# Blocks 3 to 8 in pairs, the first product by Strassen's scheme, weight operands kept in DRAM

## The chip, the cores and the metric

The kernel runs on one core of one Trainium2 chip. The metric is device microseconds of one execution. The core's engines are TensorE (PE, with its weight loads as PEld), VectorE (DVE), ScalarE (ACT), GpSimd (POOL) and SyncE (SP, which here only issues DMAs); each takes its instructions in program order and waits at an instruction until its semaphores allow it. PE writes to PSUM, eight banks of 128 x 512 fp32; DVE and ACT read and write both SBUF and PSUM.

## The reference

A linear attention feeds a gated feed-forward layer. Cut to what matters (q, k, v are 8 x 8 x 576 x 64, `d_model` is 512, `d_ff` is 1536):

```python
q_s = exp(q - max(q, -1)); q_s = q_s / (sum(q_s, -1) + 1e-09)
k_s = exp(k - max(k, 2));  k_s = k_s / (sum(k_s, 2) + 1e-09)
x = einsum('bhsd,bhde->bhse', q_s, einsum('bhsd,bhse->bhde', k_s, v))   # as [4608, 512]
xn = x / sqrt(mean(x * x, -1) + 1e-06) * rms_g
g = xn @ w_gate                                  # 512 -> 1536
out = (g * (1 / (1 + exp(-g))) * (xn @ w_val)) @ w_out   # 1536 -> 512
```

## The kernel before

The 4608 tokens are nine blocks j of 512 (`NB`, `TB`), the 1536 hidden features twelve chunks i of 128 (`NF`). A chunk of a block is a step s = 12 j + i. All three matrix products of the feed-forward layer are made in three passes over operands split in two fp32r parts, hi x hi, hi x lo and lo x hi, since one fp32r pass isn't exact enough.

For each s: `w_hi` casts the gate and val weights of the chunk (ACT, line 333), `w_lo` subtracts to get their low parts (POOL, line 811, one call for gate and one for val), `o_hi` and `o_lo` (line 819) do this for the out weights. `f1.s.0` and `f1.s.1` are gate and val: 12 matmuls each (4 slices of `d_model` x 3 passes, line 834) into one of two PSUM banks `ps_gv`. `g_mul` (DVE, line 839) multiplies the gate by the tokens' RMS factor r, `silu` (ACT, line 843) follows, `h_mul` (DVE, line 846) multiplies by val, `h_hi` (ACT) and `h_lo` (POOL, line 855) split the result, and `f2.s` (12 matmuls, line 873) adds its part of the out product to four PSUM banks `ps_o`, in which a block gathers over its 12 chunks. `store` scales by the RMS factor and writes the output. The weights come as 64-bit floats and are converted once, in block 0 (the `conv_` steps); the split into hi and lo is done anew for every s, 108 times, from the converted weights in `w_0` to `w_5`. The split tiles have two buffers each (`wsp`, `bufs=2`).

Beside this runs the attention: for batch b the `k_` steps make the 64 x 64 products of k and v, for block j the `q_` steps make softmax of q and its product with them, and the `x_` steps scale by `rms_g`, split and square the result; `n_` steps compute r. It uses two PSUM banks `ps_a`. All DMAs are issued by SP.

The order of everything is one string, `ORDER`: each word is a step with its numbers, and a letter behind a colon puts it on an engine (A is ACT, D is DVE, P is POOL). The program emits the steps in this order, and each engine gets its instructions in the order of emission.

Of the kernel before, what the change touches and what calls it, by code (L numbers as in the profile page):

```python
# [39 lines left out]
conv_low.1.0.2 n_sum0.2 conv_shift.1.1 q_max0.1.0 f1.0.0.0.2 conv_low.0.2.1 n_sum0.3 conv_sign.1.1 q_sub0.1.0:P  # L40
conv_low.2.0.2 f1.0.0.0.3 n_t.0 f1.0.1.0.0 f1.0.0.1.0 conv_add.1.0.2 f1.0.1.0.1 conv_mul.0.2 n_y0.0 f1.0.1.0.2
f1.0.1.0.3 f1.0.0.1.1 q_exp.1.0 conv_shift.0.2 f1.0.0.1.2 f1.0.0.1.3 conv_low.1.2.1 f1.0.1.1.0 n_y1.0 f1.0.1.1.1
f1.0.1.1.2 f1.0.1.1.3 f1.0.0.2.0 w_hi.1.0.2:A f1.0.0.2.1 f1.0.0.2.2 f1.0.0.2.3 f1.0.1.2.0 conv_low.3.0.2 conv_sign.0.2
w_lo.1.0:P f1.0.1.2.1 f1.0.1.2.2 f1.0.1.2.3 n_rows.0 k_tr.1.0 conv_low.2.2.1 conv_add.0.2.1 k_top.1.0 g_mul.0
# [890 lines left out]
```

## Time and profile before

| | |
|---|---|
| runs (us) | 1000.74, 1003.27, 1003.06; median 1003.06 |
| profiled execution: span | 1001.2 us |
| mean granted clock of PE | 0.997 |
| moved by DMA in the whole run | 56.71 MB on the data queue, mean 58 GB/s |
| written to DRAM | 9.44 MB |

The span is the time from the first to the last instruction of the one profiled execution; no other time of that execution is given, so the median stands 1.9 us above it for what lies around the span and for the spread of the runs. Block 0 with the loading and converting of the weights takes to about 130 us; after that a block takes 98 us plus the attention's matmuls. DMA traffic is heavy only in the first 100 us:

```profile
GB/s 236 239 305 172 116 44 88 29 52 35 44 57 42 39 1 77 47 42 16 77 35 35 35 54 57 36 35 23 65 27 9 1 43 1 1 1 42 1 1 43
```

Each number is one fortieth of the span, 25 us.

### The profile page before, as it was taken

What the parts mean: (1) busy time and instruction counts of PE and PEld (TensorE: products, weight loads), DVE (VectorE), ACT (ScalarE), POOL (GpSimd) and SP (SyncE); (2) the same over time, 40 slices, a digit from 0 to 9 for tenths busy, and PEclk for the clock granted to TensorE, in tenths of its full rate; (3) what the DMA queues carried; (4) which work ended last, traced back from release to release, by engine and by line L of the source; (5) the groups of instructions that cost most, each with busy time, mean ns of one, the idle gap of its engine ahead of it and who ended that gap; (6) DMA issues with size and microseconds to landing.
All of it is one profiled execution on the core that took longest, in us unless ns stands there. A gap on an engine that the chain in (4) does not pass through costs nothing.

```text
span 1001.2 us, 14424 instructions
## 1 busy us (share of the span) xinstructions
PE 987.5 (99%) x4897; PEld 799.2 (80%) x4897; DVE 486.6 (49%) x1170; ACT 602.7 (60%) x857; POOL 734.4 (73%) x640
## 2 busy tenths in 40 slices
PE   7999999999999999999999999999999999999998
PEld 5667878888888888888888888888888888888886
DVE  7978867654544445445444554544454322231111
ACT  5988678765765666655765666557665444434332
POOL 5688999987768786778676877777776767766663
PEclk9999999999999999999999999999999999999999
DMA  9795423121122102210211112110210010001001
GB/s 236 239 305 172 116 44 88 29 52 35 44 57 42 39 1 77 47 42 16 77 35 35 35 54 57 36 35 23 65 27 9 1 43 1 1 1 42 1 1 43
DMA packets 129686, 57.64 MB, mean 58 GB/s; under 512 B 101796, under 2 KB 123596, under 8 KB 129612
## 3 DMA queue, kind: packets, MB, share of 16 engines
q1 hardware_dynamic: 129612, 56.71, 21.7%
q8 instruction: 39, 0.64, 0.3%
q14 instruction: 35, 0.29, 0.1%
HBM read 47.25 MB, written 9.44 MB: 57 GB/s over the span
## 4 chain that ended last, share of the span: by engine, by line
PE 93%; POOL 3%; ACT 1%; DMA 1%; issue 1%; DVE 1%; SPq 0%; POOLq 0%; ACTq 0%
PE ps_gv L834 57%; PE ps_o L873 29%; PE ps_a L712 2%; PE ps_a L513 2%; POOL w L395 1%; DMA raw<-in_moe_w_out_dram 1%; PE ps_a L495 1%; DMA w<-in_k_dram 1%; POOL wl L811 0%; PE ps_a L762 0%; PE ps_a L481 0%; PE ps_a L641 0%; POOL ol L819 0%; PE ps_o L513 0%; DVE xl L734 0%
## 5 line engine op out<-in xcount | busy, mean ns | idle before, releaser
L811 POOL TENSOR_TENSOR wl<-w,wh 128x512 fp32r<-128x512 f32 x215 | 277.8, 1298 | 113.3 <-ACT wh L333 100.7
L834 PE MATMUL ps_gv<-xh,wh 128*128 128x512 f32 x864 | 346.0, 401 | 0.0
L834 PE MATMUL ps_gv<-xl,wh 128*128 128x512 f32 x864 | 336.9, 391 | 0.0
L834 PE MATMUL ps_gv<-xh,wl 128*128 128x512 f32 x864 | 231.6, 390 | 0.0
L839 DVE TENSOR_TENSOR gs<-ps_gv,r 128x512 f32<-128x512 f32 x108 | 74.6, 691 | 245.3 <-PE ps_gv L834 205.9
L834 PEld LDWEIGHTS ps_gv<-xh,wh 128*128 128x128 f32 x864 | 162.9, 189 | 36.8 <-issue 1.3
L834 PEld LDWEIGHTS ps_gv<-xh,wl 128*128 128x128 f32 x864 | 162.2, 188 | 34.9
L834 PEld LDWEIGHTS ps_gv<-xl,wh 128*128 128x128 f32 x864 | 162.9, 189 | 32.5 <-issue 0.6
L843 ACT ACTIVATE gs<-gs 128x512 f32<-128x512 f32 x108 | 68.3, 632 | 173.3 <-DVE gs L839 172.7
L873 PE MATMUL ps_o<-oh,hh 128*128 128x512 f32 x416 | 164.6, 396 | 0.0
L873 PE MATMUL ps_o<-ol,hh 128*128 128x512 f32 x416 | 162.2, 390 | 0.0
L855 POOL TENSOR_TENSOR hl<-gs,hh 128x512 fp32r<-128x512 f32 x104 | 134.5, 1293 | 28.8 <-ACT hh L333 28.3
L819 POOL TENSOR_TENSOR ol<-w,oh 128x512 fp32r<-128x512 f32 x104 | 134.6, 1294 | 16.3 <-ACT oh L333 16.3
L846 DVE TENSOR_TENSOR gs<-ps_gv,gs 128x512 f32<-128x512 f32 x108 | 74.6, 690 | 137.4 <-PE ps_gv L834 129.7
L333 ACT CAST wh<-w 128x1024 fp32r<-128x1024 f32 x103 | 108.0, 1049 | 48.8 <-PE ps_gv L834 44.7
L873 PE MATMUL ps_o<-oh,hl 128*128 128x512 f32 x416 | 111.9, 390 | 0.0
L333 ACT CAST oh<-w 128x512 fp32r<-128x512 f32 x104 | 64.0, 617 | 77.0 <-PE ps_o L873 74.7
L873 PEld LDWEIGHTS ps_o<-oh,hl 128*128 128x128 f32 x416 | 78.1, 188 | 16.7 <-POOL hl L855 0.2
L873 PEld LDWEIGHTS ps_o<-oh,hh 128*128 128x128 f32 x416 | 78.2, 188 | 16.4 <-issue 0.2
L873 PEld LDWEIGHTS ps_o<-ol,hh 128*128 128x128 f32 x416 | 78.2, 188 | 15.6 <-issue 0.2
L333 ACT CAST hh<-gs 128x512 fp32r<-128x512 f32 x103 | 64.0, 621 | 43.3 <-DVE gs L846 42.6
L843 ACT ACT_TABLE_LOAD x45 | 57.7, 1283 | 0.9
(147 smaller groups left out, 1082.8 us busy)
## 6 DMA issues: line engine op xcount, KB each, us to landing
out_dram<-ot SPq DMA_DIRECT2D x34, 256.0 KB
kt<-in_k_dram SPq DMA_DIRECT2D x28, 280.0 KB
vt<-in_v_dram SPq DMA_DIRECT2D x56, 140.0 KB
raw<-in_moe_w_gate_dram SPq DMA_DIRECT2D x7, 512.0 KB
raw<-in_moe_w_val_dram SPq DMA_DIRECT2D x7, 512.0 KB
raw<-in_moe_w_out_dram SPq DMA_DIRECT2D x7, 512.0 KB
w<-in_moe_w_gate_dram SPq DMA_DIRECT2D x5, 512.0 KB
w<-in_moe_w_val_dram SPq DMA_DIRECT2D x5, 512.0 KB
```

The costliest lines, as they stand in the source:

```text
L333: (e.copy if e is nc.scalar else e.tensor_copy)(dst, src)
L395: on(nc.gpsimd).tensor_tensor(out=dst, in0=dst, in1=raw_words(i, a, n, 0), op=ALU.add)
L513: nc.tensor.matmul(ps[h * D:(h + 1) * D, :D + 1], lhsT=ke[:n, h, j], rhs=vt[:n, j, h], start=(j == 0), stop=(j == len(rows) - 1))
L712: nc.tensor.matmul(px[:, c0:c1], lhsT=wt, rhs=mv[:, c0:c1], start=(i == 0), stop=(i == 2))
L811: on(nc.gpsimd).tensor_tensor(out=wl[:, a], in0=W(s % NF, a), in1=wh[:, a].bitcast(F32), op=ALU.subtract)
L819: on(nc.vector).tensor_tensor(out=ol, in0=W(s % NF, 2), in1=wo_[s][0].bitcast(F32), op=ALU.subtract)
L834: nc.tensor.matmul(pd[s], lhsT=m[:, a, c * P:(c + 1) * P], rhs=X[j, c][x], start=(n == 1), stop=(n == 3 * NKT))
L839: nc.vector.tensor_tensor(out=gs, in0=g_[s], in1=r_[s // NF], op=ALU.mult)
L843: nc.scalar.activation(g_[s], g_[s], AF.Silu)
L846: nc.vector.tensor_tensor(out=g_[s], in0=v_[s], in1=g_[s], op=ALU.mult)
L855: on(nc.gpsimd).tensor_tensor(out=hl, in0=g_[s], in1=h_[s][0].bitcast(F32), op=ALU.subtract)
L873: nc.tensor.matmul(po[t], lhsT=a[:, t * P:(t + 1) * P], rhs=w, start=(i == 0 and n == 0), stop=(i == NF - 1 and n == len(terms) - 1))
```

## The change

Blocks 0 to 2 are computed as before, with nearly the same steps up to s=11. Four things differ.

**Weights kept.** During blocks 1 and 2 (s=12 to s=25) the split weights are written to DRAM by SP: `w_keep` (two DMAs of 512 KB per s) and `o_keep` (two of 256 KB). For each pair of chunks four sums of weight blocks are formed, split and written too: `s_add`, `s_hi`, `s_lo`, `s_keep` (24 each, two DMAs of 256 KB each). In all 31.5 MB. Block 2 still splits its weights from `w_0` to `w_5`.

**Attention earlier.** The attention of blocks 3 and 4 is done in block 2, that of blocks 5 and 6 in pair 0, and so on, because a pair needs two blocks at once. `x_cp` makes the scaled copy, `x_nm` multiplies it by r before the product (so `g_mul` goes), and `t_add`, `b_hi`, `b_lo` build seven operands of two slices from four blocks (two halves of `d_model` x two token blocks), kept in the old weight buffers.

**Pairs.** Blocks 3 to 8 are three pairs p. A unit is a chunk pair i (of 6) and m (0 gate, 1 val). Per unit PE makes seven products `pp.p.i.m.k` of 6 matmuls in the order k = 1, 6, 5, 2, 7, 4, 3 into three PSUM banks A, B, C. A bank is read after each of its products, and the next product goes on adding to it: `c_s1` reads A after product 1, `c_u2` and `c_u3` B after 6 and 7, and `c_11`, `c_22`, `c_21`, `c_12` give the four results (two chunks x two token blocks). `gate` is the silu, `hm` the product with val, `hp_hi` and `hp_lo` the split, `f2p` the out product of one chunk and block (12 matmuls). The first block's `f2p` stands inside each unit, between products 7 and 4; the second block's twelve come one after another once the units are done. `put` stores without scaling.

**Weights read back.** In the pairs no weight is split. POOL issues DMAs that read the kept operands: per unit `w_in` part 1 (1 MB, line 1068, 128 x 2048) and part 2 (768 KB, 128 x 1536), and `o_in` (512 KB, line 1080) for each `f2p`; 144 DMAs. Part 1 has one buffer per m, part 2 one per m, the out weights four.

What moves is shown by the instruction rows of before and of the changed kernel (lines are those of each kernel's own file). On PE, the end of one chunk's first product and the start of an out product, near the end of before:

```order
L834 MATMUL ps_gv<-xl,wh 128x512
L834 MATMUL ps_gv<-xh,wl 128x512 [waits Pool_49]
L834 MATMUL ps_gv<-xh,wl 128x512 x3
L873 MATMUL ps_o<-oh,hh 128x512 [waits Activation_49]
L873 MATMUL ps_o<-ol,hh 128x512 [waits Pool_49]
```

And on PE in pair 1 of the changed kernel, products 5, 2, 7 of one unit and the `f2p` in it (`x_` tiles hold the operands, `ring_` tiles and `w` the weights read back, DMASW is a DMA issued by POOL):

```order
L1095 MATMUL ps_o<-x_4437,w 128x512 [waits DVE_49]
L1095 MATMUL ps_o<-x_4437,w 128x512 x5
L1095 MATMUL ps_o<-x_4199,w 128x512 [waits Activation_49]
L1095 MATMUL ps_o<-x_4199,w 128x512 x5
L1095 MATMUL ps_o<-x_4199,ring_3487 128x512 [waits DMASW3_49,DVE_49]
L1095 MATMUL ps_o<-x_4199,ring_3487 128x512
L1095 MATMUL ps_o<-x_4444,ring_3487 128x512 x2
L1095 MATMUL ps_o<-x_4199,ring_3487 128x512
L1095 MATMUL ps_o<-x_4444,ring_3487 128x512
L1182 MATMUL ps_a<-x_4170,hh 128x512 [waits DMASW5_49]
```

PE's waits for POOL's and ACT's weight splits are gone; in their place stand waits for DMAs and, at each product, for DVE or ACT having read the bank.

On POOL in block 1, a chunk or so before the change (`wl`, `ol`, `hl` are low parts, `qt` and `ql` attention):

```order
L811 TENSOR_TENSOR wl<-w_92,wh 128x512 [waits PE_49,Activation_49,Pool_49]
L855 TENSOR_TENSOR hl<-gs,hh 128x512 [waits Activation_49]
L811 TENSOR_TENSOR wl<-w_92,wh 128x512
L819 TENSOR_TENSOR ol<-w_92,oh 128x512 [waits Activation_49,Pool_49]
L664 TENSOR_TENSOR qt<-qt,st 128x512 [waits DMAHW3_49,DMAHW4_49,DMAHW2_49,DMAHW5_49,DMAHW1_49,DMAHW6_49,DMAHW0_49,DMAHW7_49,DVE_49,Pool_49]
```

And after it (line 877 is `w_lo`, 885 `o_lo`, 975 `h_lo`, 927 `s_add`, 936 `s_lo`; DMAHW is a DMA issued by SP):

```order
L975 TENSOR_TENSOR hl<-gs,hh 128x512 [waits Activation_49]
L936 TENSOR_TENSOR parts<-sums,parts 128x2x256 [waits DMAHW4_49,DMAHW3_49,Activation_49]
L877 TENSOR_TENSOR w<-w_93,w 128x2x256 [waits DMAHW1_49,DMAHW2_49,PE_49,Activation_49]
L516 MEMSET vt 116x10 [waits DMAHW6_49,DMAHW5_49,DMAHW7_49,DMAHW0_49,PE_49]
L936 TENSOR_TENSOR parts<-sums,parts 128x2x256 [waits DMAHW6_49,DMAHW5_49,Activation_49]
L885 TENSOR_TENSOR o<-w_92,o 128x512 [waits Activation_49]
L877 TENSOR_TENSOR w<-w_93,w 128x2x256 [waits DMAHW7_49,DMAHW0_49,Activation_49]
L877 TENSOR_TENSOR w<-w_93,w 128x2x256
L927 TENSOR_TENSOR sums<-sums,w_93 128x512
```

`s_add` and `s_lo` have come between the splits, and a split waits for the stores that read its buffer.

On DVE at the start of pair 0 (line 966 is `h_mul`, 733, 707, 737, 715 attention, 589 a reciprocal, 1014 `x_nm`, 1039 `t_add`, 1051 `b_lo`); in before this place has no such rows:

```order
L966 TENSOR_TENSOR gs<-ps_gv,gs 128x512 [waits PE_49,Activation_49]
L733 SCALAR_TENSOR_TENSOR sm<-sm,sw 128x16 [waits DVE_49]
L589 RECIPROCAL rs<-rs 128x1
L707 TENSOR_REDUCE sw<-st 32x16 x4
L737 RECIPROCAL sm<-sm 128x16 [waits DVE_49]
L715 TENSOR_TENSOR st<-st,sw 128x16 [waits DVE_49]
L1014 TENSOR_TENSOR xl<-xl,r 128x512
L1039 TENSOR_TENSOR ot<-xl,xh 128x512 [waits Pool_49] x2
L1039 TENSOR_TENSOR xl<-xl 128x512 [waits DVE_49,Pool_49]
L1039 TENSOR_TENSOR xl<-xl 128x512 [waits DVE_49]
L1039 TENSOR_TENSOR xh<-xl,xh 128x512 [waits DVE_49] x2
L1051 TENSOR_TENSOR x_4437<-ot,x_4437 128x512 [waits Activation_49]
```

The rows after it are four more of `b_lo`; PE's product 6 of the first unit waits for the third `b_lo`. Three of the four `x_nm` of block 4 stand on POOL.

The diff, cut to its core; of the `ORDER` string one line each of a late stretch is shown:

```diff
-store.6.3:A f1.86.0 h_mul.85 w_hi.87.0.2:A h_hi.85:A w_lo.87.0:P h_lo.85:P f2.84 g_mul.86 silu.86 w_lo.87.1:P f1.86.1
...
+c_u2.1.3.0 pp.1.3.0.2 pp.1.3.0.7 c_11.1.3.0 w_in.1.4.0.1 f2p.1.0.4 c_u3.1.3.0 c_22.1.3.0 gate.1.3.22 pp.1.3.0.4
...
+    wsp = ctx.enter_context(tc.tile_pool(name="wsp", bufs=2))
+    big = ctx.enter_context(tc.tile_pool(name="big", bufs=1))
...
+    S2, S1, A11, A12, A21, A22, S3, S4 = range(8)
+    wd = [[tc.dram_tile([P, 8, 2, HALF], F32, name=f"wd{i}_{m}") for m in range(2)] for i in range(NH)]
+    od = [tc.dram_tile([P, 2, DM], F32, name=f"od{i}") for i in range(NF)]
+    def w_keep(s):
+        i, odd = divmod(s % NF, 2)
+        at = A21 if odd else A11
+        for m in range(2):
+            nc.sync.dma_start(wd[i][m][:, at:at + 2], wh_[s][:, m].bitcast(F32))
+    def s_add(i, n):
...
+        c = turn["sums"] = turn.get("sums", -1) + 1
+        sums[i, n] = parts[0][:, c % 6]
+        x, y, op = {1: (a(1, 0), a(1, 1), ALU.add), 2: (sums.get((i, 1)), a(0, 0), ALU.subtract),
+                    3: (a(0, 0), a(1, 0), ALU.subtract), 4: (a(0, 1), sums.get((i, 2)), ALU.subtract)}[n]
+        on(nc.vector).tensor_tensor(out=sums[i, n], in0=x, in1=y, op=op)
+    def x_nm(j, g):
+        x = XF[(j - JP) % 2, g]
+        on(nc.vector).tensor_tensor(out=x, in0=x, in1=r_[j], op=ALU.mult)
+    def t_add(p, n, c):
...
+        o, x, y, op = {1: (T1.get(c), b, a, ALU.subtract), 3: (b, e, b, ALU.subtract), 2: (a, b, a, ALU.add),
+                       4: (d, d, a, ALU.subtract)}[n]
+        on(v).tensor_tensor(out=o, in0=x, in1=y, op=op)
+    def b_lo(p, o, c):
+        on(nc.gpsimd).tensor_tensor(out=operand(o, c, 1), in0=source(o, c), in1=operand(o, c, 0).bitcast(F32),
+                                    op=ALU.subtract)
+    def w_in(p, i, m, part):
+        ring()
+        if part == 1 and m == len(RING[1]):
+            RING[1].append(wsp.tile([P, 4, TB], F32R, name="w"))
+        t = RING[part][m].rearrange("p a b -> p (a b)")
+        src = wd[i][m][:, :4] if part == 1 else wd[i][m][:, 5:]
+        nc.gpsimd.dma_start(t, src.rearrange("p a b f -> p (a b f)"))
+    def o_in(p, t, c):
...
+        nc.gpsimd.dma_start(WO[n % 4], od[c])
+    PROD = {1: (A11, 0, 0), 6: (S2, 1, 1), 5: (S1, 2, 2), 2: (A12, 3, 0), 7: (S3, 4, 1), 4: (A22, 5, 1), 3: (S4, 6, 2)}
+    def pp(p, i, m, k):
+        w, o, b = PROD[k]
+        first = k in (1, 6, 5)
...
+        terms = [(0, c, x) for c in range(2) for x in range(2)] + [(1, c, 0) for c in range(2)]
+        for n, (h, c, x) in enumerate(terms):
+            nc.tensor.matmul(abc[b], lhsT=src[:, h, c * P:(c + 1) * P], rhs=operand(o, c, x),
+                             start=first and n == 0, stop=n == 5, skip_group_check=not first)
+    def combine(u, n, dst, src, b):
+        ux[u + (n,)] = dst
+        nc.vector.tensor_tensor(out=dst, in0=ux[u + (src,)], in1=abc[b], op=ALU.add)
+    def hm(p, i, n):
+        t = cell(p, i, n)
+        on(nc.vector).tensor_tensor(out=t, in0=t, in1=ux[p, i, 1, n], op=ALU.mult)
+    def f2p(p, t, c):
...
+        (hh, hl), (oh, ol) = HH[p, t, c], wo_[p, t, c]
+        terms = ((hh, oh), (hh, ol), (hl, oh))
+        order = [(n, k) for k in range(T) for n in range(2)] + [(2, k) for k in range(T)]
...
+    def put(p, t, n):
+        ot = fp.tile([P, DM], F32, name="ot", bufs=2)
+        copy(ot, pa[p, t, n], nc.vector if n % 2 else nc.scalar)
+        nc.sync.dma_start(ov[blk(p, t), n], ot)
```

More of the change, by code (lines that the diff above doesn't have):

```diff
@@ L40 @@
[L40 to L44, printed above, removed]
@@ L380, in conv_mul @@
     def conv_mul(i, a):
-        cv[i, a] = ps_a.tile([P, TB], F32, name="ps_a")
+        cv[i, a] = ps("attn")
         nc.scalar.mul(cv[i, a], raw_words(i, a, 1, 1).bitcast(F32), 2.0 ** -112)
@@ L397, in warm @@
     def warm(n, _=0):
-        out = ps_gv.tile([P, TB], F32, name="ps_gv")
+        out = ps("gv")
         for _ in range(n):
@@ L407, in attn_ps @@
     def attn_ps(first):
-        if first:
-            return ps_o.tile([P, TB], F32, name="ps_o")
-        return ps_a.tile([P, TB], F32, name="ps_a")
+        return ps("o" if first else "attn")
     kt_, vt_, ke_, mb_, cm_, kps, rs_, kv, kx_, kd_ = {}, {}, {}, {}, {}, {}, {}, {}, {}, {}
@@ L759, in n_sum @@
     def n_sum(j):
-        pm = ps_a.tile([P, TB], F32, name="ps_a")
+        pm = ps("attn")
         for i, a in enumerate(dg_[j]):
@@ new lines, in w_in @@
+    def w_in(p, i, m, part):
[6 more added lines that the diff above has]
+    def o_in(p, t, c):
+        ring()
+        n = turn["wo"] = turn.get("wo", -1) + 1
+        while len(WO) < 4 and n >= len(WO):
+            if len(WO) == 1:
+                operand(6, 1, 1)
+                WO.append(XO[4][:, 4:6])
+            else:
+                WO.append(wsp.tile([P, 2, DM], F32R, name="o"))
+        wo_[p, t, c] = [WO[n % 4][:, k] for k in range(2)]
+        nc.gpsimd.dma_start(WO[n % 4], od[c])
@@ new lines, in linear_attention_then_gated_ffn, with h2, c_s1 @@
+    ux = {}
+    def h2(c):
+        if c not in H2:
+            if c < 8:
+                H2[c] = xp.tile([P, TB], F32, name=("xh", "xl")[c // 4])
+            else:
+                t = wsp.tile([P, 4, TB], F32, name="w")
+                for k in range(4):
+                    H2[8 + k] = t[:, k]
+        return H2[c]
+    def c_s1(p, i, m):
+        t = ux[p, i, m, 1] = tmp("s")
+        copy(t, abc[0], nc.scalar)
+    def combine(u, n, dst, src, b):
+        ux[u + (n,)] = dst
+        nc.vector.tensor_tensor(out=dst, in0=ux[u + (src,)], in1=abc[b], op=ALU.add)
@@ new lines, in h_src, with hp_hi, hp_lo @@
+    def h_src(p, t, c):
+        return h2(c) if t else g_[p, c]
+    def hp_hi(p, t, c):
+        hh = fp.tile([P, TB], F32R, name="hh", bufs=2)
+        copy(hh, h_src(p, t, c), nc.scalar)
+        HH[p, t, c] = [hh]
+    def hp_lo(p, t, c):
+        hl = fp.tile([P, TB], F32R, name="hl", bufs=2)
+        on(nc.gpsimd).tensor_tensor(out=hl, in0=h_src(p, t, c), in1=HH[p, t, c][0].bitcast(F32), op=ALU.subtract)
+        HH[p, t, c].append(hl)
+    pa = {}
+    def f2p(p, t, c):
+        if c == 0:
+            if t and p + 1 < NPAIR:
+                attn_pool[0] = BANKS[p % 2][1][3]
+            for n in range(T):
+                pa[p, t, n] = ps(BANKS[p % 2][1 - t][n])
+        (hh, hl), (oh, ol) = HH[p, t, c], wo_[p, t, c]
+        terms = ((hh, oh), (hh, ol), (hl, oh))
+        order = [(n, k) for k in range(T) for n in range(2)] + [(2, k) for k in range(T)]
+        if c == NF - 1:
+            order.sort(key=lambda x: (x[1], x[0]))
+        for n, k in order:
+            a, w = terms[n]
+            nc.tensor.matmul(pa[p, t, k], lhsT=a[:, k * P:(k + 1) * P], rhs=w, start=(c == 0 and n == 0),
+                             stop=(c == NF - 1 and n == 2))
```

719 lines of the change are left out of this document (435 added, 284 removed).

## The prediction, made before the changed kernel had run

> **What bounds the kernel now.** I read the head of the page first, then its chain, then the chain's rows in order of time, then stretches of the run.
>
> ```profile
> span 1001.2 us, 14424 instructions
> PE 987.5 (99%) x4897; PEld 799.2 (80%) x4897; DVE 486.6 (49%) x1170; ACT 602.7 (60%) x857; POOL 734.4 (73%) x640
> PE 93%; POOL 3%; ACT 1%; DMA 1%; issue 1%; DVE 1%; SPq 0%; POOLq 0%; ACTq 0%
> ...
> 904.76 8.16 PE ps_gv L834 x36
> ...
> 986.36 5.44 PE ps_gv L834 x24
> ```
>
> TensorE (PE) is busy for 99% of the span and makes 93% of the chain that ends last. The chain rows give its pace: 36 matmuls in 8.16 us, so 0.2267 us each, and one feature chunk of a block (24 matmuls at L834, 12 at L873) takes 8.16 us. The stretches say what lies under it (columns: length, busy us of PE, PEld, DVE, ACT, POOL, then granted clock, DMA share, GB/s).
>
> ```profile
> 0.00:50.00 50.00, 42.74 (x234) 28.11 (x234) 40.52 (x97) 37.67 (x62) 29.18 (x52) 0.97 0.90 237
> 50.00:60.00 10.00, 8.02 (x47) 6.25 (x47) 7.10 (x13) 6.99 (x13) 7.66 (x6) 0.83 0.88 253
> 60.00:70.00 10.00, 10.00 (x38) 6.74 (x37) 8.43 (x14) 8.69 (x13) 7.57 (x8) 1.00 1.11 334
> 70.00:80.00 10.00, 10.00 (x40) 6.91 (x39) 9.16 (x15) 9.48 (x13) 10.00 (x8) 1.00 1.01 336
> 130.00:228.00 98.00, 98.00 (x509) 80.18 (x507) 62.56 (x168) 73.86 (x102) 88.78 (x78) 1.00 0.22 50
> 228.00:326.00 98.00, 98.00 (x510) 80.46 (x509) 50.86 (x130) 60.57 (x85) 73.20 (x63) 1.00 0.19 46
> 326.00:620.00 294.00, 294.00 (x1510) 241.36 (x1509) 141.20 (x373) 182.17 (x255) 216.86 (x186) 1.00 0.18 43
> ```
>
> From 130 us on PE has no gap at full clock. But in block 1 (about 130 to 228) POOL is already busy for 88.78 of 98 us, in block 2 for 73.20. So matmuls removed come off the end in full, while vector work added to blocks 1 and 2 meets a nearly full POOL.
>
> **The change part by part.** *Matmuls removed.* The first product of blocks 3 to 8 is 6 blocks x 12 chunks x 24 = 1728 matmuls; as seven half-size products it is 3 pairs x 12 units x 7 x 6 = 1512. 216 fewer x 0.2267 us = **-49.0 us**. The second product stays at 12 matmuls per chunk and block.
>
> *Vector work of the pairs.* In blocks 3 to 8 the three weight splits of each chunk go (three POOL operations of 1.30 us); per unit of 54 matmuls (12.24 us on PE) DVE now has some eight operations and POOL one or none.
>
> ```profile
> L811 POOL TENSOR_TENSOR wl<-w,wh 128x512 fp32r<-128x512 f32 x215 | 277.8, 1298 | 113.3 <-ACT wh L333 100.7 <-ACT hh L333 7.5 <-PE ps_a L762 3.1
> L846 DVE TENSOR_TENSOR gs<-ps_gv,gs 128x512 f32<-128x512 f32 x108 | 74.6, 690 | 137.4 <-PE ps_gv L834 129.7 <-PE ps_a L481 5.9 <-ACT wh L333 0.9
> L686 POOL TENSOR_TENSOR qt<-qt,sm 128x512 f32<-128x512 f32 x28 | 29.5, 1054 | 16.3 <-DVE sm L683 9.6 <-DVE rs L535 6.8
> L811 DVE TENSOR_TENSOR wl<-w,wh 128x512 fp32r<-128x512 f32 x1 | 0.7, 689 | 0.0
> ```
>
> Eight at 0.69 us are 5.5 of 12.24 us: PE covers them in pairs 1 and 2, and between a bank's last matmul and its next user lie two products, 2.72 us, for a read of 0.69. Cost nothing there. In pair 0 the attention of blocks 5 and 6 is added: counted with the row means, DVE has 135 us in eleven units of 151 us of PE, and over PE's time in four of them (2.0 us together). With the five build-up stages beside the second products, where x_nm and t_add make the next operands (about 4 us over), I take **+6**; the ends are 0 and 10.
>
> *Blocks 1 and 2 with the weights kept.* Here DVE and POOL disturb each other:
>
> ```profile
> 128.62 1.31 POOL L855 TENSOR_TENSOR hl<-gs,hh 128x512 fp32r<-128x512 f32 x1
> ...
> 129.21 1.27 DVE L739 TENSOR_TENSOR acc<-acc,sq 128x512 f32<-128x512 f32 x1
> ...
> 129.91 1.71 POOL L811 TENSOR_TENSOR wl<-w,wh 128x512 fp32r<-128x512 f32 x1
> ```
>
> The DVE sum of two SBUF tiles, 0.69 us alone, starts under a POOL operation and ends only 0.55 us after it; the POOL operation begun meanwhile takes 1.71 instead of 1.30. So the two kinds run as one queue. In block 1 (from the first product of s=12 to that of s=24) the new order has on POOL 68 such operations x 1.30 and 6 x 1.05 = 94.7 us, and on DVE 32 with two SBUF inputs x 0.69 = 22.1: 116.8 us against 106.8 of PE. That is 0 (if PE's work lies well around it) to 10; I take **+8**, since two weight buffers let POOL run only one chunk ahead. In block 2, 64 x 1.30 + 12 x 1.05 + 14 x 0.69 = 105.5 against 110.3, but DVE as a whole has 104.8, and in its first two chunks 25.4 against 22.4 of PE: 3.0, and as much again for the 14 shared operations waiting half a POOL operation (0.65, 9 us, a third of which has no slack): **+6**, ends 0 and 17 (the sum of every chunk's excess).
>
> The Trainium skill, "SBUF — State Buffer", section "Who interferes with whom", says that a DVE operation with two SBUF inputs and a POOL operation reading SBUF hold one port pair by turns and block each other; the trace agrees (1.27 against 0.689 us). Taken strictly, and for DVE casts too, it is the third case below.
>
> *The stores.* 31.5 MB leave over s=12 to 25, some 128 us: 246 GB/s, with the attention's 50 about 296. Loads reached 334 to 336, so I cost them nothing; the other end is the 237 of the first 50 us: 38 MB in 160 us, +32. SP issues 195 DMAs there:
>
> ```profile
> 61.44 4.00 SPq L455 DMA_DIRECT2D vt<-in_v_dram  x4
> ...
> 66.14 0.40 SPq L369 DMA_DIRECT2D w<-in_moe_w_gate_dram  x1
> ...
> 998.40 0.33 SPq L888 DMA_DIRECT2D out_dram<-gs  x1
> ```
>
> 0.33 to 1.0 us each, 64 to 195; near the middle row, which is a weight tile's (0.40 to 0.5), 90 of 128, hidden. Two waits are new. On SP the attention's loads stand behind a store that waits for its split; they come a chunk or more before use. On POOL a split waits until the store of two chunks earlier has read its buffer; behind it stands `h_lo`, for which the out product on PE waits. With some eight DMAs on the way at 88% of the rate a store is late now and then: that is in the +8 of block 1, whose cover is one chunk, 8.16 us.
>
> *The start of pair 0.* Product 6 needs both blocks normalised and added. From the end of the first product's gate half at s=35 DVE has in its queue: two PSUM products, two transposes, a sum, eight quarter moves and six small steps, then x_nm, six t_add and three b_lo.
>
> ```profile
> L839 DVE TENSOR_TENSOR gs<-ps_gv,r 128x512 f32<-128x512 f32 x108 | 74.6, 691 | 245.3 <-PE ps_gv L834 205.9 <-PE ps_a L481 15.3 <-POOL wl L811 13.4
> L691 DVE STREAM_TRANSPOSE qT<-qt 128x512 f32<-128x512 f32 x28 | 19.6, 702 | 1.3 <-POOL qt L686 1.2
> L672 DVE TENSOR_REDUCE sm<-qt 128x16 f32<-128x512 f32 x28 | 19.0, 679 | 15.6 <-ACT qt L668 15.6
> L653 DVE TENSOR_REDUCE sw<-sm 32x16 f32<-32x16 f32 x112 | 18.0, 161 | 2.1
> L535 DVE RECIPROCAL rs<-rs 128x1 f32<-128x1 f32 x32 | 4.9, 153 | 0.7
> L679 DVE SCALAR_TENSOR_TENSOR sm<-sm,sw 128x16 f32<-128x16 f32 x28 | 8.4, 299 | 0.3
> L683 DVE RECIPROCAL sm<-sm 128x16 f32<-128x16 f32 x28 | 7.1, 252 | 0.6
> ```
>
> 2 x 0.69 + 2 x 0.70 + 0.68 + 8 x 0.16 + 0.30 + 2 x 0.25 + three of about 0.16 = 6.0, and ten two-input operations x 0.69 = 6.9: ready 12.9 us on. PE has the value half (2.72) and product 1 (1.36), 4.1 us, so it stands for about 9. A stand is followed by slow matmuls:
>
> ```profile
> 56.28 0.86 PE L628 MATMUL ps_a<-ident,xl 128*128 128x128 f32 x4 [1.98 <-ACT ot L338]
> 56.80 0.77 PE L834 MATMUL ps_gv<-xh,wh 128*128 128x512 f32 x1
> ...
> 60.20 0.63 PE L834 MATMUL ps_gv<-xh,wl 128*128 128x512 f32 x2
> ```
>
> Eight matmuls in 3.40 us instead of 1.81, at a granted clock of 0.83 in that stretch: 1.6 more. Together **+10.7**; 4 if the steps before s=35 run ahead, 13 if POOL blocks half of those ten.
>
> *Weights read back.* POOL issues 144 DMAs, three per unit (2.36 MB in 12.24 us, 193 GB/s) and one of 0.52 MB per 2.72 us beside the second products, the same rate. No row shows a DMA issued by POOL: between nothing and SP's 1.0 us each, at most 3 of 12.24 us on a POOL that else has 1.3. I take nothing, because the rate is 58% of 334 to 336 and a buffer is refilled a unit ahead. The Trainium skill, "DMA: Bandwidth & Descriptors", section "Measured (HBM→SBUF, 128 partitions, SWDGE, issued from GpSimd)", gives 6.15 us and 341 GB/s for 1 MB; by it the term is nothing too, and no run here has shown it yet.
>
> *The end.* The last stores wait for the last matmuls as before: 0.
>
> **The sum:** 1001.2 - 49.0 + 8 + 6 + 10.7 + 6 = 982.9 by the span. The median of the runs, 1003.06, is 1.9 above the span: **985 us**, its own range 970 to 998.
>
> **The rivals.** *PE alone bounds:* the stalls hide, since the same PE queue had no gap beside a POOL at 91%; only part of the start of pair 0 is left. 1003.1 - 49.0 = 954, plus 0 to 14: 954 to 968. Against it stands the 12.9 us queue.
>
> *One queue of DVE and POOL throughout:* block 1 +12, block 2 +17, start +13, pair 0 and the build-ups +8: 1003.1 - 49 + 50 = 1004 at most, 996 to 1006 likely. For it: the stretched rows above. Against: in block 1 of before POOL and PE shared 98 us without a stop.
>
> *The read-back is too slow (slower than before):* all of the pairs' 104 MB come by POOL's queue while DVE and POOL work, and PE waits for a weight tile in each unit. PE needs 539 us for the pairs' weight matmuls; 104 MB in 560 us, 186 GB/s, is where the forecast passes 1006. At half the seen rate, 167, they take 622: 83 more, 1068. The Trainium skill, "SBUF — State Buffer", same section, warns that POOL's descriptor writing starves while DVE holds the pair; no row here shows it.
>
> *The products do not keep the pace:* 252 short groups with changing banks, each followed by a read. 18 us over 252 (0.07 us each) eats the gain; at 0.25, as in the few groups beside attention that take 2.97 instead of 2.72, it is 63 us and 1048.
>
> ```profile
> 723.62 2.97 PE ps_gv L834 x12
> 727.56 2.75 PE ps_gv L834 x12
> ```
>
> Against it: runs of 24 and 36 matmuls cross banks at 0.2267.
>
> **How the numbers follow.** Forecast 0.50, PE alone 0.17, one queue 0.18, slow read-back 0.11, lost pace 0.04. The forecast and PE alone are nearly all faster by over 0.3% (below 1000.0, about what a measurement here can tell from no change); the one-queue case is a third faster, two fifths the same, the rest slower; the last two slower. Faster 0.70, same 0.11, slower 0.19. A range from 954 to 1008 leaves out the last two cases and a little of the third, and covers the stores' dearer end (985 + 32 less the 14 already in blocks 1 and 2 = 1003).
>
> **What would show it.** PE busy near 938 us, 4,680 or so matmuls; PE at 2.72 us per 12 in pairs 1 and 2 with no gap named after a DMA; in blocks 1 and 2 gaps of PE ended by POOL or DVE (w_lo, g_mul, q_x inputs), some 14 us; one gap near 9 us at the first L1095 of pair 0, ended by DVE L1051, with a clock below 1 after it. A PE that waits for L1068 or L1080 loads in every unit would make it wrong, as would POOL rows of several us at L1068.

## The result, and the profile after

The changed kernel takes **1041.68 us** (median; 1037.83 to 1045.3) beside 1001.9 us of the kernel before on the same chip: a ratio of 1.0392, 95% interval 1.0358 to 1.0426. It is slower by about 39 us. The forecast was 985 us with a range of 954 to 1008: both the direction and the range were wrong.

The head of its page, and the first line of its chain:

```profile
span 1042.5 us, 14185 instructions
PE 971.2 (93%) x4681; PEld 773.5 (74%) x4681; DVE 739.7 (71%) x1460; ACT 467.3 (45%) x705; POOL 574.8 (55%) x575
PE 56%; DVE 20%; DMA 10%; issue 5%; POOL 3%; ACT 3%; SPq 3%; DVEq 0%; POOLq 0%; ACTq 0%
```

The 216 matmuls are gone (4897 to 4681). Their 49.0 us should have brought PE's busy time from 987.5 to 938.5; it is 971.2, since matmuls at half clock last longer (mean granted clock 0.967, before 0.997). And PE stands (has no matmul under way) for 1042.5 - 971.2 = 71.3 us, before for 13.7, which is 57.6 more. So the balance is -49.0 + 32.7 of slow matmuls + 57.6 of standing = +41.3 us of span. In the chain PE's share has fallen from 93% to 56%.

By stage (blocks 1 and 2, then the three pairs; columns as in the prediction: stretch, length, busy PE, PEld, DVE, ACT, POOL, granted clock, DMA share, GB/s), the changed kernel:

```profile
148.00:413.00 265.00, 240.51 (x1254) 191.11 (x1253) 228.23 (x477) 161.25 (x224) 204.38 (x175) 0.94 0.59 187
413.00:649.00 236.00, 214.76 (x1093) 171.92 (x1092) 192.69 (x429) 120.49 (x184) 141.59 (x145) 0.96 0.69 188
649.00:849.00 200.00, 189.22 (x823) 154.97 (x820) 114.56 (x189) 44.76 (x76) 72.50 (x84) 0.97 0.60 185
849.00:1042.00 193.00, 186.22 (x818) 152.80 (x816) 84.88 (x131) 24.96 (x41) 35.35 (x52) 1.00 0.57 177
```

PE stands for 24.5 us in blocks 1 and 2, for 21.2 in pair 0 and for 10.8 in pair 1, each time with a clock below 1. By the forecast the units of pair 1 should have had no gap. DVE is busy for 228 of 265 us in the first stage; in blocks 1 and 2 of before it had 113 of 196, less than ACT and POOL.

**What holds PE up.** The waits view of the changed kernel (engine, tile and line <- what it waited for: us in all, times, longest) has four rows on one tile, the buffer through which a block's result leaves:

```profile
DVE ot L389 <- DMA out_dram<-ot: 21.4, 5, 5.7
ACT ot L389 <- DMA out_dram<-ot: 21.4, 4, 9.6
...
DVE ot L396 <- DMA out_dram<-ot: 14.5, 4, 7.5
...
ACT ot L394 <- DMA out_dram<-ot: 13.8, 3, 6.0
```

These are 71 us in 16 waits, of two engines whose waits overlap in part. The group of these copies in before (count, busy us, mean ns, idle time of ACT ahead of them and what ended it) had waited 1.2 us for such a store:

```profile
L338 ACT ACTIVATE ot<-ps_o,yt 128x512 f32<-128x512 f32 x33 | 21.4, 680 | 4.5 <-PE ps_o L873 3.2 <-DMA out_dram<-ot 1.2
```

Here is one of the places, the four output copies of block 2 in pair 0 of the changed kernel (timeline: start, length, engine, line, operation, count, and in brackets the idle time before it and what ended that):

```profile
450.59 3.78 SPq L635 DMA_DIRECT2D qt<-in_q_dram  x8
...
451.12 0.68 ACT L394 ACTIVATE ot<-ps_o,yt 128x512 f32<-128x512 f32 x1
451.30 0.75 DVE L396 TENSOR_SCALAR ot<-ps_o,yt 128x512 f32<-128x512 f32 x1
...
454.47 4.63 SPq L998 DMA_DIRECT2D out_dram<-ot  x4
457.38 0.69 ACT L394 ACTIVATE ot<-ps_o,yt 128x512 f32<-128x512 f32 x1 [5.58 <-DMA out_dram<-ot]
457.99 0.75 DVE L396 TENSOR_SCALAR ot<-ps_o,yt 128x512 f32<-128x512 f32 x1 [5.37 <-DMA out_dram<-ot]
458.66 0.68 DVE L1116 TENSOR_TENSOR tmp<-tmp,ps_gv 128x512 f32<-128x512 f32 x1
...
459.39 2.93 PE L1095 MATMUL ps_gv<-x,ring 128*128 128x512 f32 x6 [6.19 <-DVE tmp L1116]
```

There are two `ot` buffers. The first two copies fill them at 451; the stores are issued from 454.47 on (SP is at the loads of q until then), and the first has landed at 457.38. Until then ACT and DVE stand at the third and fourth copy. Behind DVE's copy in its queue is the read of the bank (L1116) for which PE's next product waits: PE stands 6.19 us. The copies of one block in before, on ACT's timeline:

```profile
374.52 1.25 ACT L338 ACTIVATE ot<-ps_o,yt 128x512 f32<-128x512 f32 x2
...
378.19 0.67 ACT L338 ACTIVATE ot<-ps_o,yt 128x512 f32<-128x512 f32 x1
...
382.33 0.69 ACT L338 ACTIVATE ot<-ps_o,yt 128x512 f32<-128x512 f32 x1
```

There were two buffers there as well, but the third and the fourth copy came 2.4 and 3.5 us after the one ahead of them, with other work of ACT between, and DVE had none of them.

Two explanations follow from this. **The output buffers**: they make PE stand at the end of each block or pair, and the slow clock follows. **The weights' load**, which the forecast may have priced too low: the weights' stores and sums load SP, the DMA engines, DVE and POOL in blocks 1 and 2. The experiments take them apart. (The expectations below give letters to their theories, each text its own; in the first one "Theory A" is the output buffers.)

### The profile page after: what moved, and what is told of

It reads as the page before. It is cut to its first block, busy times and chain, and to the rows that moved or that the text cites. A ratio compares the mean times of both kernels' runs of the same rounds, so it can differ in the third digit from the quotient of the medians.

```text
span 1042.5 us, 14185 instructions
## 1 busy us (share of the span) xinstructions
PE 971.2 (93%) x4681; PEld 773.5 (74%) x4681; DVE 739.7 (71%) x1460; ACT 467.3 (45%) x705; POOL 574.8 (55%) x575
## 4 chain that ended last, share of the span: by engine, by line
PE 56%; DVE 20%; DMA 10%; issue 5%; POOL 3%; ACT 3%; SPq 3%; DVEq 0%; POOLq 0%; ACTq 0%
PE ps_gv L1095 13%; PE ps_o L1095 10%; PE ps_gv L954 8%; PE ps_o L1182 8%; PE ps_a L1095 5%; PE ps_o L991 3%; PE ps_a L1182 3%; DMA out_dram<-ot 3%; PE ps_gv L1182 3%; DMA vt<-in_v_dram 2%; DVE hh L389 2%; DMA qt<-in_q_dram 2%; DVE tmp L1116 1%; SPq L635 1%; DVE sw L707 1%
## 5 line engine op out<-in xcount | busy, mean ns | idle before, releaser
L954 PE MATMUL ps_gv<-xh,w 128*128 128x512 f32 x576 | 198.7, 412 | 3.7 <-DVE gs L959 2.0
L1095 PE MATMUL ps_gv<-x,ring 128*128 128x512 f32 x576 | 150.1, 406 | 14.8 <-DVE tmp L1116 8.8
L1095 PEld LDWEIGHTS ps_gv<-x,ring 128*128 128x128 f32 x576 | 110.4, 195 | 40.5 <-DVE tmp L1116 10.3
L954 PEld LDWEIGHTS ps_gv<-xh,w 128*128 128x128 f32 x576 | 112.6, 196 | 31.4 <-DVE gs L966 2.3
L954 PE MATMUL ps_gv<-xl,w 128*128 128x512 f32 x288 | 116.6, 408 | 0.0
L1116 DVE TENSOR_TENSOR tmp<-tmp,ps_gv 128x512 f32<-128x512 f32 x84 | 57.3, 683 | 48.5 <-PE ps_gv L1095 47.0
L877 POOL TENSOR_TENSOR w<-w,w 128x512 fp32r<-128x512 f32 x61 | 82.4, 1360 | 10.2 <-ACT w L389 5.0
L1095 PE MATMUL ps_o<-x,ring 128*128 128x512 f32 x360 | 86.8, 394 | 0.0
L1095 PEld LDWEIGHTS ps_o<-x,ring 128*128 128x128 f32 x360 | 68.6, 191 | 14.6
L991 PE MATMUL ps_o<-o,hh 128*128 128x512 f32 x256 | 66.5, 401 | 3.1 <-ACT hh L389 2.6
L1080 POOL DMA_DIRECT2D o<-od x36 | 20.5, 571 | 66.4 <-PE ps_o L1182 37.6
L1116 DVE TENSOR_TENSOR tmp<-tmp,ps_o 128x512 f32<-128x512 f32 x42 | 28.7, 685 | 30.0 <-PE ps_o L1095 29.4
L1068 POOL DMA_DIRECT2D w<-wd x18 | 10.0, 555 | 60.6 <-PE ps_a L1095 35.8
L975 POOL TENSOR_TENSOR hl<-gs,hh 128x512 fp32r<-128x512 f32 x24 | 32.3, 1344 | 18.4 <-ACT hh L389 16.8
L1182 PE MATMUL ps_o<-o,hh 128*128 128x512 f32 x144 | 38.2, 398 | 2.6 <-DVE hh L389 2.6
```

What stands on the lines that cost most here:

```text
L877: on(nc.gpsimd).tensor_tensor(out=w[:, :, 1], in0=halves(s % NF, a, 1)[:, 0], in1=w[:, :, 0].bitcast(F32), op=ALU.subtract)
L954: nc.tensor.matmul(pd[s], lhsT=w[:, a, c // 2, m, c % 2 * P:c % 2 * P + P], rhs=X[j, c][x], start=(n == 1), stop=(n == 3 * NKT))
L975: on(nc.gpsimd).tensor_tensor(out=hl, in0=g_[s], in1=h_[s][0].bitcast(F32), op=ALU.subtract)
L991: nc.tensor.matmul(po[t], lhsT=a[:, t * P:(t + 1) * P], rhs=w, start=(i == 0 and n == 0), stop=(i == NF - 1 and n == len(terms) - 1))
L1068: nc.gpsimd.dma_start(t, src.rearrange("p a b f -> p (a b f)"))
L1095: nc.tensor.matmul(abc[b], lhsT=src[:, h, c * P:(c + 1) * P], rhs=operand(o, c, x), start=first and n == 0, stop=n == 5, skip_group_check= ...
```

## The experiments

In the table, "stands" is span less PE's busy time and "slow" is that busy time less 938.5, both of the profiled execution; ratio and interval are against runs of the kernel before on the same chip. In e7_warm and e8_all the busy time has 24 added matmuls in it, so some 5.4 us of their "slow" are work and not clock.

| run | median us | ratio (95%) | stands | slow |
|---|---|---|---|---|
| changed kernel | 1041.68 | 1.0392 (1.0358 to 1.0426) | 71.3 | 32.7 |
| e1_ot4 | 1007.71 | 1.0088 (1.0052 to 1.0124) | 49.8 | 16.6 |
| e2_nostore | 1036.54 | 1.0355 (1.0312 to 1.0399) | 69.8 | 29.6 |
| e3_nosums | 1031.42 | 1.0304 (1.0279 to 1.0329) | 69.1 | 22.7 |
| e4_neither | 1029.85 | 1.0288 (1.0262 to 1.0315) | 69.4 | 19.1 |
| e10_spread | 1019.95 | 1.0183 (1.0167 to 1.0198) | 58.4 | 21.5 |
| e12_actq | 1045.79 | 1.0438 (1.0410 to 1.0465) | 80.2 | 25.3 |
| e6_hpA | 1000.91 | 1.0019 (0.9992 to 1.0047) | 45.9 | 14.2 |
| e9_allA | 996.46 | 0.9943 (0.9922 to 0.9964) | 43.0 | 13.8 |
| e7_warm | 1009.04 | 1.0079 (1.0049 to 1.0109) | 46.4 | 22.2 |
| e5_back | 1019.98 | 1.0191 (1.0164 to 1.0218) | 65.0 | 15.4 |
| e8_all | 1016.95 | 1.0178 (1.0148 to 1.0208) | 53.7 | 21.6 |
| e11_oback | 1004.74 | 1.0034 (1.0018 to 1.0049) | 48.4 | 13.0 |
| e13_f2 | 997.07 | 0.9944 (0.9922 to 0.9966) | 40.7 | 12.3 |
| e14_six | 997.73 | 0.9960 (0.9939 to 0.9982) | 40.4 | 13.5 |
| e15_nosums | 987.32 | 0.9852 (0.9831 to 0.9874) | 35.8 | 11.4 |

### Output buffers: four, later copies, another queue

e1_ot4, the whole edit (at four places):

```diff
-        ot = fp.tile([P, DM], F32, name="ot", bufs=2)
+        ot = fp.tile([P, DM], F32, name="ot", bufs=4)
```

> Changed kernel with four buffers instead of two for the output tiles (ot). Theory A, late output stores: ACT and DVE stand at an output copy until the store of two copies earlier has landed, and PE loses 8.6 us at s=13 and 14, 9.0 in unit 0.1.0 and 9.2 in unit 1.1.0 (idle and slow clock together). The three waits go and the time falls by 20 to 27 us, to about 1015 to 1022. Rival B, DVE is behind in any case: the waits are taken over by what stands next in its queue, the three gaps shrink by less than a third, 1033 or more.

1007.71 us, 34 less by the medians and 30 less by the ratios, which is more than the expected 20 to 27. The slow clock fell with the gaps (32.7 to 16.6), and of the 71 us of waits for output stores 1.6 are left. The stages of e1_ot4:

```profile
149.00:400.00 251.00, 233.27 (x1255) 186.34 (x1253) 226.47 (x478) 161.08 (x225) 204.25 (x175) 0.97 0.63 198
400.00:627.00 227.00, 210.79 (x1087) 168.79 (x1088) 193.22 (x426) 120.09 (x184) 138.58 (x145) 0.98 0.72 195
627.00:816.00 189.00, 186.47 (x828) 152.64 (x824) 114.39 (x190) 44.75 (x76) 71.52 (x84) 1.00 0.63 197
816.00:1005.00 189.00, 184.91 (x816) 152.78 (x814) 85.24 (x131) 25.16 (x41) 35.35 (x52) 1.00 0.58 179
```

All four stages gain: 14, 9, 11 and 4 us. The expectation had counted three gaps of 8.6, 9.0 and 9.2 us, slow clock and all; the excess lies in blocks 1 and 2 and in pair 2. The gaps at 170, 459 and 686 us of the changed kernel are gone. This is the largest part of the error.

e10_spread keeps two buffers and moves the third and fourth copy of each block some steps back in `ORDER`, one of its moves being:

```diff
-q_sum2.5.3 store.2.2:A store.2.3:D
+q_x.5.2 store.2.2:A
...
+q_load.6.2 store.2.3:D
```

> Changed kernel with its two output buffers, but the third and fourth output copy of each block moved later in the order of steps, about half and nine tenths of the way to the step that needs their PSUM bank (the last block's stay). If the order of steps is what made the buffers too few (copies in a row, where before had 5 us between the second and the third): most of the 34 us of four buffers, 1010 to 1018. If two buffers are too few with these loads and stores whatever the order: 1028 or more.

1019.95 us: two thirds of e1_ot4's gain, and 2 us short of the expected range. The waits for output stores fall from 71 to 32 us. So the greater part comes from the distance between the copies, which before had and the change lost. Before also had these copies on ACT alone; what that alone is worth was not tried.

e12_actq lets ACT issue the output stores, so that they don't stand behind SP's loads of q and k:

```diff
-        nc.sync.dma_start(dst, ot)
+        nc.scalar.dma_start(dst, ot)
```

> Changed kernel with its two output buffers, the 36 output stores issued by ACT instead of SP. In the trace of the changed kernel the first two copies of block 2 end at 452.0 but SP, busy with eight loads of q, issues their stores at 454.5, and the third copy starts at 457.4. If the queue on SP is most of the wait: the gap of 6.2 us there falls to about 3, that of unit 1.1.0 from 7.1 to about 5, time 1028 to 1034. If the time to land is most of it: 1036 to 1042, or slower, as ACT's own work waits behind each issue.

1045.79 us, nothing gained; PE still stands for 6.41 us at the place shown above. Its second store and its fourth copy there:

```profile
453.43 0.34 ACTq L998 DMA_DIRECT2D out_dram<-ot  x1
...
458.43 0.75 DVE L396 TENSOR_SCALAR ot<-ps_o,yt 128x512 f32<-128x512 f32 x1 [5.61 <-DMA out_dram<-ot]
```

The stores leave 1 to 2 us earlier than from SP, yet DVE's copy starts 5.0 us behind the issue of the store that it waits for. So SP's queue, with the loads at 450.59, is not what decides at this place: with two buffers the time until a store has landed is enough.

### The weights' stores and the sums

e2_nostore leaves out the stores of the split weights for chunk pairs 1 to 5, e3_nosums their sums, e4_neither both; in all three the pairs read chunk pair 0's operands in their place, so that the work of the pairs stays as it was and blocks 3 to 8 come out with wrong weights.

```diff
+        if i:
+            return
...
-        src = wd[i][m][:, :4] if part == 1 else wd[i][m][:, 5:]
+        src = wd[0][m][:, :4] if part == 1 else wd[0][m][:, 5:]
```

> Changed kernel without the weight stores of chunk pairs 1 to 5 (all of the splitting and summing stays; the pairs read chunk pair 0's weights every time, the same bytes). Theory A: with 26 of 31.5 MB not written the output stores of block 0 land in time, the gap of PE at 170 us goes (8.6 us), those in pairs 0 and 1 stay: 1030 to 1034. Theory C, DVE and POOL block each other: the stalls of s=23 to 25 (13.4 us) stay. Rival D, the splits wait for their buffers' stores: most of the 38 us that blocks 1 and 2 lost go, 1003 to 1010.

> Changed kernel without forming, splitting and storing the sums of chunk pairs 1 to 5 (60 steps of DVE, POOL and ACT and 10.5 MB less; the weights of every chunk are still kept; the pairs read chunk pair 0's weights every time). Theory C, DVE and POOL as one queue: some 52 us of shared work less in s=12 to 25, PE's stalls there fall by 15 to 25 us, 1017 to 1027. Rival D (stores): about a third of what the run without stores gains. Rival E, the attention's order and its late loads: under 6 us.

> Changed kernel without the sums and without the weight stores of chunk pairs 1 to 5. Theories A and C together: idle and slow clock of PE from s=12 to s=35 fall from 38 us to under 10, 1008 to 1014. Rival E (attention moved ahead, with its loads and its DVE work in block 2): s=26 to s=35 keeps its 10 us, and s=12 to 25 another 10 or more, 1020 or more.

Without the stores 1036.54 us: its interval overlaps that of the changed kernel, so the traffic of the weights costs little or nothing. Without the sums 9 us less by the ratios, with neither 10. That refutes the weights' load as the main cause (it would have to be worth over 30 us) and leaves the sums a smaller one.

### Casts between DVE and POOL

DVE's casts are stretched. Rows of the changed kernel's timeline around a small operation with two SBUF inputs, and around one of the casts:

```profile
487.82 2.85 DVE L733 SCALAR_TENSOR_TENSOR sm<-sm,sw 128x16 f32<-128x16 f32 x1
...
488.09 1.30 POOL L802 TENSOR_TENSOR ql<-acc,qh 128x512 fp32r<-128x512 f32 x1
489.34 1.28 POOL L755 TENSOR_TENSOR ql<-qT,qh 128x512 fp32r<-128x512 f32 x1
...
670.17 3.11 DVE L389 CAST hh<-gs 128x512 fp32r<-128x512 f32 x1
670.44 1.30 POOL L755 TENSOR_TENSOR ql<-qT,qh 128x512 fp32r<-128x512 f32 x1
671.70 1.30 POOL L1014 TENSOR_TENSOR xh<-xh,r 128x512 f32<-128x512 f32 x1
```

A cast that before had once on DVE, in 0.41 us, takes 3.11: it ends 0.28 us after the second of two POOL operations in a row, as the small operation ends 0.05 us after such a second one. The groups (count, busy us, mean ns) of this one cast, before:

```profile
L333 DVE CAST hh<-gs 128x512 fp32r<-128x512 f32 x1 | 0.4, 414 | 0.0
```

and in the changed kernel:

```profile
L389 DVE CAST hh<-gs 128x512 fp32r<-128x512 f32 x30 | 26.8, 895 | 0.6
```

e6_hpA is e1_ot4 with the 44 casts `hp_hi` that stood on DVE put on ACT, e9_allA with all 85 (`w_hi`, `o_hi`, `s_hi`, `h_hi` and others):

```diff
-hp_hi.0.0.0:D
+hp_hi.0.0.0:A
```

> Four output buffers, and all 72 casts of the pairs' results (hp_hi) on ACT, 44 of which stood on DVE. Theory C: DVE's casts stretch from 0.41 to 0.7 us on the mean because POOL works; taken off DVE, pair 0's idle time (16.2 us, 6.0 of them at its start) falls by 3 to 6 us and the idle time of 1 to 2 us beside the second products goes: 1001 to 1005. Rival: PE isn't waiting for them: 1006 to 1009.

> Four output buffers, all casts of the pairs' results on ACT (as in e6_hpA), and the other casts that stood on DVE (of weights, sums, hidden results, q and x: 35 in blocks 0 to 2 and pair 0) on ACT too. Theory C, PE waits for a DVE that is stretched by POOL: idle and slow clock in s=12 to 35, 23.5 us with e6_hpA, fall by 6 to 12, time 990 to 996. Rival H, ACT becomes the late one (9.8 of 9.4 us of PE in s=17): 1001 to 1006, gaps ended by ACT.

1000.91 and 996.46 us. e9_allA's interval of the ratio lies below 1: the change, with these two amendments, is faster than the kernel before by 0.6%. Its first three stages:

```profile
151.00:395.00 244.00, 230.69 (x1256) 186.26 (x1255) 199.09 (x442) 181.23 (x260) 201.37 (x175) 0.98 0.65 204
395.00:621.00 226.00, 210.11 (x1078) 168.32 (x1078) 182.87 (x418) 127.23 (x197) 138.21 (x144) 0.98 0.73 196
621.00:806.00 185.00, 184.97 (x833) 152.78 (x830) 101.27 (x168) 54.85 (x93) 71.57 (x85) 1.00 0.65 200
```

Beside e1_ot4, DVE lost 27 us in blocks 1 and 2 and ACT took 20; the stage is 7 us shorter, and pair 1 has no gap left. Over the whole run DVE's busy time falls from 738.6 to 681.1 us, 0.68 per cast, so more than the casts take alone. Whether it is the stretching or the mere number of DVE's operations that PE waited for, these two runs do not tell.

### The start of pair 0

e7_warm is e1_ot4 with 24 matmuls on constants ahead of the first product 6, so that PE's clock stays up while it waits:

```diff
+            if (p, i, m, k) == (0, 0, 0, 6):
+                for _ in range(24):
+                    nc.tensor.matmul(abc[b], lhsT=mean_w, rhs=mean_w.unsqueeze(1).broadcast_to([P, T, P]), start=True, stop=True)
```

> Four output buffers, and 24 matmuls without use (5.4 us at 0.2267) in the bank of product 6 ahead of the first product 6, where PE stands for 5.7 us. Theory G, the stand itself halves the clock: no half clock around 400 us, the slow-clock loss of unit 0.0.0 (2.1 us) goes, time 1005 to 1006. Rival: the extra matmuls run past the end of the wait and cost as much as they bring: 1007 to 1009.

The product's 11 matmuls behind the wait take 4.35 us in e1_ot4's timeline,

```profile
408.17 4.35 PE L1095 MATMUL ps_gv<-x,ring 128*128 128x512 f32 x11 [0.36 <-DVE x L1051]
```

and 2.94 in e7_warm's:

```profile
410.28 2.94 PE L1098 MATMUL ps_gv<-x,ring 128*128 128x512 f32 x11 [0.65 <-DVE x L1051]
```

PE still waits 0.65 us behind the added matmuls, so they don't run past the end of the wait. Yet the run is no shorter (1009.04; the ratio is 1.0079 beside 1.0088). What PE wins there it loses again within pair 0, which takes 227 us in both. So "slow" in the table can be more than what the clock costs.

### Block 2 with its weights read back

e5_back (on e1_ot4) drops the second splitting: block 2 reads hi and lo back by POOL, gate, val and out; e11_oback (on e6_hpA) only out; e8_all is e5_back, e6_hpA and e7_warm together.

```diff
+    def w_back(s):
...
+        for m in range(2):
+            nc.gpsimd.dma_start(w[:, m], wd[i][m][:, at:at + 2])
```

> Four output buffers, and block 2 (s=24 to 35) reads its split weights back from DRAM by POOL's queue instead of splitting them anew (24 casts of ACT or DVE and 36 subtractions, most on POOL, less; 36 DMAs more). Theory C, DVE and POOL as one queue: idle and slow clock of PE in s=23 to 35, 16.2 us with four buffers alone, fall below 8, and the time to 998 to 1001. Rival E, the attention moved ahead into block 2 is what DVE is late with: 1006 to 1009, the gaps stay. Rival F, POOL stands at a DMA whose buffer PE still uses, and h_lo behind it comes late: above 1009.

> As e6_hpA, and block 2 reads only the out weights back (12 DMAs of 512 KB; 12 casts and 12 subtractions less), the gate and val weights are split as before. If e5_back lost by the third more traffic that its 36 DMAs put before the attention's small loads (DVE stood 9.4 us for one): a third of the traffic takes back more than it costs, 996 to 1000. If any DMA on POOL in block 2 holds up what is queued behind it: 1002 to 1008.

> The last three edits together on four output buffers. If they act on separate stalls: 992 to 999, below before. If they share a cause: no better than the best of them alone.

None of the hoped-for gains came: 1019.98, 1004.74 and 1016.95 us. POOL's and ACT's work fell, but the loads of the attention are late. In e5_back's timeline:

```profile
339.19 14.62 SPq L634 DMA_DIRECT2D qt<-in_q_dram  x16
...
351.22 0.69 DVE L700 TENSOR_REDUCE st<-qt 128x16 f32<-128x512 f32 x1 [9.40 <-DMA qt<-in_q_dram]
```

DVE waits 9.40 us for them, and PE stands 9.74 us behind it. The same 16 loads in e1_ot4 were issued in 12.07 us, and DVE waited 2.25:

```profile
327.64 12.07 SPq L635 DMA_DIRECT2D qt<-in_q_dram  x16
```

The four loads of v ahead of them took 8.05 us in e5_back and 2.90 in e1_ot4. From 245 to 345 us e5_back's DMA share is 1.00 (296 GB/s), in e1_ot4 from 245 to 332 it is 0.64 (200 GB/s). That the added reads are the reason fits these figures. Rival F, POOL standing at a buffer that PE still uses, may have a part: POOL waits there for 2.86 and 2.26 us.

### What is left: PE's order, or the load

e13_f2 and e14_six move out products that were ready ahead of the step at which PE stood in e9_allA; e15_nosums is e9_allA without the sums of chunk pairs 1 to 5.

```diff
-b_lo.0.2.1:D pp.0.0.0.6
+b_lo.0.2.1:D f2.34 pp.0.0.0.6
```

> The run e9_allA (four output buffers, casts on ACT, 996.5 us) with one step moved: f2.34, the out product of the last but one chunk of block 2, stands ahead of product 6 of the first pair unit instead of behind product 5. It gives PE 2.72 us of work in the gap of some 6 us in which PE waits for the operands of product 6. Theory 'PE's order': the gap shrinks by 2.7 us, the half clock behind it (1.85 us) may go too: 992 to 994. Theory 'capacity of DVE and POOL': the operand arrives when it arrives and all that follows is late with it, PE then waits for the next thing: 995.5 to 997.

> The run e9_allA with six out products moved ahead of the attention step at which PE stood: f2.34 as in e13_f2, f2.23 ahead of q_x.3.0, f1.30.1 ahead of q_x.4.0, f2.29 ahead of k_tr.4.3, f1.33.0 ahead of k_rows.5.0, f1.34.1 ahead of k_mm.5.0. If PE's order alone makes it stand (work was there, but queued behind a late attention step), the idle time and slow clock from s=12 to the first unit fall from 26 us to 16 or less: 986 to 991. If DVE and POOL have too much to do in these blocks, the gaps come back at the next steps: 993 to 998.

> The run e9_allA without the sums, their splits and their stores for chunk pairs 1 to 5; the pairs read the operands of chunk pair 0 in their place, so blocks 3 to 8 come out with wrong weights. POOL loses some 20 splits and 10 or so sums of 1.3 us in blocks 1 and 2, DVE the rest of the sums. If the sums' load on DVE and POOL makes PE stand in blocks 1 and 2, idle and slow clock from s=12 to 35 fall from 18 to under 6 us: 982 to 986. If PE's order does it, they stay above 12: 990 to 996.

997.07 and 997.73 us: nothing, as "capacity" has it. In e13_f2 PE stands 3.28 instead of 5.95 us at product 6, and the time doesn't move. Without the sums 987.32 us, 9 less by the ratios (their stores, left out too, are in it). The first stage of e15_nosums:

```profile
148.00:387.00 239.00, 229.39 (x1256) 185.45 (x1255) 186.37 (x433) 171.16 (x240) 159.94 (x145) 0.99 0.54 164
```

It is 5 us shorter than e9_allA's and PE stands 9.6 instead of 13.3 us: less than expected, between the two theories. The sums' load is some 9 us; 9.6 us of standing in blocks 1 and 2 and 15.0 in pair 0 remain without them. Attention that runs a block earlier and the build of pair 0's operands are the likely reasons; that was not taken apart.

## Why the prediction was wrong, point by point

*What bounds the kernel and the matmuls removed: right.* -49.0 us came off PE's full-clock work. In pairs 1 and 2 of the changed kernel PE keeps the pace in stretches in which no output store is waited for:

```profile
700.00:760.00 60.00, 60.00 (x266) 49.68 (x265) 29.88 (x50) 8.88 (x15) 17.03 (x22) 1.00 0.61 192
900.00:960.00 60.00, 60.00 (x266) 49.71 (x265) 26.61 (x41) 9.43 (x17) 10.29 (x17) 1.00 0.62 191
```

60 / 266 = 0.2256 us per matmul, next to the 0.2267 of before. So the rival **lost pace** is refuted.

*Weights read back at nothing: right.* Three rows of the changed kernel, first two of its DMA list (KB each, median us to land):

```profile
ring<-wd POOLq DMA_DIRECT2D x36, 768.0 KB, 5.0
ring<-wd POOLq DMA_DIRECT2D x18, 1024.0 KB, 5.3
```

and of its groups the issue on POOL:

```profile
L1068 POOL DMA_DIRECT2D ring<-wd x54 | 30.0, 556 | 109.4 <-PE ps_o L1095 42.9
```

0.556 us to issue, 5.3 us to land 1 MB, a unit of 12.24 us ahead; no wait of PE names such a load, at 191 GB/s. The rival **slow read-back** is refuted; its time, 1068, was nearer to the result than the forecast, as was lost pace with 1048, for reasons that aren't there.

*The stores at nothing, and the end at nothing: here it failed.* I priced the 31.5 MB of weights, rightly at about nothing (e2_nostore). But of the output stores I looked at the last ones alone. That the step order puts a block's four output copies close together, and that `ot` has two buffers, was in the code and appears in no term: copies and their stores stood at nothing, as in before, where only 1.2 us were waited for one. Measured by e1_ot4: 34 us by the medians, of the 57 missed the larger part.

*The slow clock: priced once, 1.6 us, in the start of pair 0.* What the row at 56 us of before showed, slow matmuls behind a stand, should have been weighed for each gap that I forecast. Busy time over 938.5 is 32.7 us in the changed kernel and 16.6 with four buffers. That is the most the clock can have cost: e7_warm took part of it away and was no shorter.

*Blocks 1 and 2: +8 and +6, too small.* With four buffers PE stands 17.7 us there, and the clock is 0.97; with the casts on ACT 13.3, without the sums 9.6. I gave the shared port 14 operations of DVE in block 2, those with two SBUF inputs, and none of its casts, which e6_hpA and e9_allA show to cost, over the whole run, 7 and another 8 us by the ratios. The Trainium skill, "SBUF — State Buffer", section "Who interferes with whom", lists copy and cast among what can take the shared port pair and block, where their operands allow it; the prediction named that as part of the third case. The stretched casts agree with it (3.11 against 0.41 us), and the small operation of 2.85 us with its two-input rule. So the rival **one queue** was nearer in this stage (29 us against 14). But it isn't POOL that is full there (204 of 265 us) but DVE (228), part of whose busy time is itself such stretching.

*The start of pair 0: +10.7, near in size, and partly by luck.* PE stands 5.68 and 0.36 us at the first product 6 of pair 0, 6.0 where 9 were forecast, with half clock behind it:

```profile
420.00:425.00 5.00, 4.12 (x9) 2.93 (x10) 4.81 (x9) 1.07 (x2) 5.00 (x1) 0.50 0.07 11
```

The half clock lasts until about 427: 6.5 us of work at half speed, so 3.3 us lost where 1.6 were forecast, 9.3 in all. The two errors nearly cancel. And the longer wait ends with ACT's cast (`b_hi`), where the forecast had DVE's L1051 (`b_lo`). In e7_warm and e13_f2 filling this gap brought no time back.

*The inside of pair 0 and the build-up stages: +6, about half of what came.* With four buffers PE stands 16.2 us in pair 0, 10 of them behind its start; pair 1 has 2.5, and pair 2 4.1 with the tail of the run in it.

By spans 59.6 us were missed (1042.5 against 982.9). 37.6 of them go with the output buffers (e1_ot4), which no term had. The other 22.0 are stalls that the forecast had, too small: 9.6 go with the casts on DVE (e9_allA) and 9.6 with the sums (e15_nosums); by the ratios these three are 30, 14 and 9.
